# Zero rows by one write and two DMA copies, one weight piece ahead of the list reads, and one gather behind a weight piece

## The chip, the cores and the metric

The kernel runs on one core of one Trainium2 chip. The metric is the device time of one execution in microseconds (us), lower is better. Three executions of the kernel before took 493.13, 488.73 and 491.85 us; the median is 491.85 us.

## The reference

A gated linear attention (4 batches, 8 heads, 768 steps, head size 48) with a complex decay, and on its output, seen as 3072 tokens of 384 values, a mixture of 8 experts. Each token goes to one expert only:

```python
logits = x @ w_gate
e_idx = np.argmax(logits, axis=1)
...
for e in range(E):
    mask = e_idx == e
    h = np.maximum(x[mask] @ w1[e], 0.0)
    ye = h @ w2[e]
    out[mask] = gate_w[mask, None] * eom[mask, e, None] * ye
```

Here w1[e] is 384x1024 and w2[e] is 1024x384, both float32.

## The kernel before, in words

**Attention.** The 3072 tokens are 24 tiles of 128. A long text, `ORDER`, names every step of this part one by one (`sc.20.1`, `mk.20.1`, ...), and the instructions of all engines are recorded in that order; each engine then runs its own in that order and waits on semaphores. A tile's finished rows go to a table `xd` in DRAM (step `xs`, line 723, SP's queue).

**Routing.** In four batches the tokens get a place in their expert's list. `pl` computes addresses on POOL (GpSimd) with seven small operations (lines 1024 to 1031), `el` writes 20 of the 24 tiles' entries to a DRAM table by indirect DMA (line 1035). The last four tiles are placed in SBUF instead. The experts are taken in order of their size, so which expert comes first is known only at run time (`who`, a register on SP).

**Weights.** An expert's weights come in four pieces of 768 KB (`piece`, line 296: w1 first half, w2 first half, w1 second half, w2 second half) into three staging buffers `raw`. Each piece is split in three steps into a rounded high part (`w1h`, `w2h`, a cast on ACT) and the rest (`w1l`, `w2l`, a subtraction on DVE). A buffer is free for the next piece when DVE has done its third subtraction. All piece loads and all reads of the lists stand on SP's one queue, which waits at its head.

**Rows.** A gather (line 1089) is four indirect DMAs issued by POOL that bring an expert's token rows from `xd` into `rows[e % 2]`. Lists may be shorter than the room for them, so `open_` (line 783) first zeroes both `rows` tiles, four 128x384 memsets each on POOL (line 791). PE turns the rows (`transpose_x`), ACT and DVE split them into `xh` and `xl`.

**Experts.** For each expert `e` eight rounds `ft` follow. In a round PE makes 9 up products (line 1176, into bank `b` or `xo` by turns), ACT takes the relu `hh` (line 1272), DVE the rest `hl` (line 1273), and one round later PE makes 9 down products from them (line 1191). By hand-written numbers each round also takes some steps of a chain of work for the next expert (`steps`: six splits of the first expert's last two pieces, twelve splits of the second's, the issue of the third's pieces, three turned row tiles). In the first expert's rounds another chain (`last`, the function `lists`) enters the last four tiles into all experts' lists: compare rows `hot`, gates, a product (line 862) and its copy `by_slot`, then additions to `slots` and `whole`, the row numbers `sid`, and the second expert's gather. The lists of the experts 2 to 8 are read from DRAM by SP (`read_ranked`: six reads at line 1056, four at line 1062) just after the first expert's fourth piece is asked for. Line 1161 is the branch that picks a matmul width for an expert at run time; line 186 is the helper of all transposes.

Of the kernel before, what the change touches and what calls it, by code (L numbers as in the profile page):

```python
# [21 lines left out]
P = 128  # L22
# [85 lines left out]
va.19 xn.18v rnd.23a cq.20.0v xs.18 fr.23 dk.22 abs.23a st.19 qc.22 xt.19 sin.23 trk.20.0 sd.19 cos.23 trk.20.1  # L108
ck.20.0v cq.21.1 trq.22.0 cps.19v ck.20.1 ro.19 kc.21 cq.21.0 open set.16 sc.20.1 gt.19 qc.23 sc.20.0 mk.20.1
trk.21.0 R1.3 trk.21.1 ck.21.0 st.20 ck.21.1v rk.3 R3.3 sc.21.1 R2.3 Ae.3 sd.20 pl.3 sc.21.0 R4.3 cps.20 mk.21.1  # L110
st.21 el.3 mk.21.0 mk.20.0 trq.23.1 trq.23.0 kc.22 trq.22.1 kc.23 va.20 xn.19v K2 chk xs.19 trk.22.1 xt.20 sd.21
trk.23.1 cq.22.1 ck.22.1v va.21 cps.21 K3 ck.23.1 cq.22.0 K4 sc.22.1 xt.21 cq.23.1v KV trk.22.0 cq.23.0v
trk.23.0 mk.22.1 wd sc.23.1 ck.23.0 rr ck.22.0v lw.2 wr sc.23.0 mk.23.1 lw.0 sc.22.0 mk.23.0 ro.20 si mk.22.0 ga
ro.21 xh.20 gt.20 xn.20 xl.20 va.22 xh.21 xs.20 gt.21 P1.0 xn.21 xs.21 xl.21 st.22 xt.22v PK.0 sd.22 ro.22 P2.0
# [9 lines left out]
def tile_gated_attention_moe(  # L124
# [13 lines left out]
    nc = tc.nc  # L138
# [3 lines left out]
    HD = H * D  # L142
# [3 lines left out]
    N = B * S  # L146
# [140 lines left out]
    def one(w, e):  # L287
        return w[e] if isinstance(e, int) else w[bass.ds(e, 1)].rearrange("o a b -> (o a) b")

    def piece(stage, e, n, since=None):  # L290
        t = stage.tile([P, KT * FH], F32, name="raw")
        if n % 2 == 0:
            src = one(w1, e).rearrange("(k p) f -> p k f", p=P)[:, :, n // 2 * FH:(n // 2 + 1) * FH]
        else:
            src = one(w2, e).rearrange("(k p) f -> p k f", p=P)[:, n // 2 * TH:(n // 2 + 1) * TH, :]
        ins = nc.sync.dma_start(out=t.rearrange("p (k f) -> p k f", f=src.shape[2]), in_=src)
        if since is not None:
            behind(ins, since)
        return t
# [139 lines left out]
    def attention(wctx, pp):  # L439
        with ExitStack() as actx:  # L440
# [342 lines left out]
            def open_():  # L783
                ectx.close()
                ready["stage"] = wctx.enter_context(tc.tile_pool(name="stage", bufs=3, side="right", reuse_waits="tile"))
                pool = wctx.enter_context(tc.tile_pool(name="wset0", bufs=1, side="right", reuse_waits="tile"))
                ready["pool"], ready["set"] = pool, weight_set(pool)
                for n in range(2):
                    rows[n] = pool.tile([P, NS, HD], F32, name=f"rows{n}")
                    for i in range(NS):  # L790
                        nc.gpsimd.memset(rows[n][:, i, :], 0.0)
                for name, dt in (("dl", F32), ("oh", BF16), ("ohp", F32)):
                    tail[name] = pool.tile([P, NT - T0, E], dt, name=name + "s")
                ready["x"] = [pool.tile([P, KT, CAP], F32R, name=n) for n in ("xh0", "xl0")]

            def lw(n):
# [143 lines left out]
            def late():  # L940
# [11 lines left out]
                rk=rk, R2=R2, R3=R3, Ae=Ae, R4=R4, pl=pl, el=el, K1=K, K2=K, K3=K, K4=K, KV=K, chk=chk, wd=wd, wr=wr, open=open_,  # L952
                lw=lw, sa=sa, sb=sb, rr=rr, si=si, ga=ga, P1=PK, PK=PK, P2=PK, tl=tl, th=th, fl=fl, cn=cn, cv=cv)
            for name, f in (("y", y), ("z", z), ("u", u)):
# [25 lines left out]
            with tc.manual_schedule(engines={mybir.EngineType.SP, mybir.EngineType.Pool}):  # L980
                for name, a, moved in todo:
# [3 lines left out]
                    if whose:  # L985
                        left[whose] -= 1
                        if not left[whose]:
                            free.append(held[whose])
            for ins in read_ranked(1, E):
                behind(ins, tail["gathered"])  # L990
# [95 lines left out]

    def gather(e, cap, known=N, loaded=True):
        for i, (t, n) in enumerate(tiles_at(e, cap, loaded)):
            ins = nc.gpsimd.indirect_dma_start(  # L1089
                out=rows[e % 2][:n, i, :], out_offset=None, in_=xd[:known],  # L1090
                in_offset=bass.IndirectOffsetOnAxis(ap=id_of(e, i, n, loaded), axis=0),
                bounds_check=known - 1, oob_is_err=False)
        return ins


    def experts(ready, loaded=False):
# [4 lines left out]
        with ExitStack() as ectx:  # L1101
# [14 lines left out]
            turns_of = [*part, *hidden, sums, done_rows, *bank_of.values()]  # L1116
            X, W, L = {}, {}, {}

            def across(e, columns):
# [16 lines left out]
            def weights(e):  # L1136
                W[e] = wsets[e % 2]
                if e + 1 < E and e not in L:
                    L[e] = pieces_of(e)
# [109 lines left out]
            for e in range(E):  # L1249
                if e + 1 < E and not (loaded and e == 0):  # L1250
                    gather(e + 1, sizes[e + 1], loaded=loaded)
                steps = itertools.chain(ready["late"]() if loaded and e == 0 else (), ahead(e + 1))
                accs, cap = None, sizes[e]
                for ft in range(FT):
# [3 lines left out]
                    if loaded and e == 0 and ft < 2:  # L1258
                        if before is not None:
                            by_width(e, down_products(*before))  # L1260
                    elif loaded and e == 0 and ft == 3:
                        by_width(e, up_products(e, ft, up))
# [28 lines left out]
                    if loaded and e == 0:  # L1291
                        for _ in range((0, 2, 1, 0, 0, 0, 0, 0)[ft]):
                            next(last)
# [5 lines left out]
                        if ft >= 4:  # L1299
                            next(flags, None)  # L1300
                    for _ in range((0, 0, 4, 4, 4, 4, 3, 3)[ft] if loaded and e == 0 else 3):
                        next(steps, None)
# [221 lines left out]
```

## Time and profile before

| | |
|---|---|
| median of 3 runs | 491.85 us (488.73 to 493.13) |
| profiled execution, its own time | 492.66 us |
| its span, first to last instruction | 490.9 us |
| around the span | 1.76 us |
| mean granted TensorE clock | 0.990 |
| busy share PE, DVE, ACT, POOL | 95%, 70%, 62%, 27% |

The profile is one execution. Its views: a page with busy time by engine and by slice, the chain of waits that ended last, the timeline of each engine (start, duration, in brackets the idle time before and what ended it), and windows with each engine's busy time, the granted clock and the DMA engines' share. Attention ends near 250 us of the span, the first expert's rounds run from there to about 282 us, the other seven experts to 482 us.

### The profile page before, as it was taken

To read this page: it belongs to the slowest core of one execution; us is meant where nothing else is said; L and a number is where in the kernel's file an instruction comes from. 1 tells how busy PE (TensorE), PEld (TensorE's weight loads), DVE (VectorE), ACT (ScalarE), POOL (GpSimd) and SP (SyncE) were. 2 spreads that over 40 slices of the span, in tenths; PEclk is the share of its full clock that TensorE was granted. 3 is DMA by queue.
4 is the path that set the end of the run, shared out by engine and by line. 5 is a ranking of instruction groups with operands and counts; after the bars stand their busy time and mean duration, and the time that the engine had idled before them with its cause. 6 is when DMAs were issued, how large, how long until landed. Compare 5 with 4: busy or idle time off the path is not lost.

```text
span 490.9 us, 11411 instructions
## 1 busy us (share of the span) xinstructions
PE 465.4 (95%) x4350; PEld 419.6 (85%) x4350; DVE 342.7 (70%) x694; ACT 303.5 (62%) x569; POOL 132.4 (27%) x168
## 2 busy tenths in 40 slices
PE   8998999899999999989899789999999999999991
PEld 4786777788988789879799689999999999999991
DVE  4599999999999999998798564272644527283210
ACT  7759889989997987542536464372744636283330
POOL 5100000013700640582404543324241322011112
PEclk9999999999999999998999999999999999999997
DMA  8974354534633331002636996274452827220001
GB/s 278 316 232 132 99 159 126 168 91 102 122 129 99 78 72 50 18 4 76 229 86 221 241 246 200 63 229 131 138 180 51 284 61 232 80 91 26 22 27 49
DMA packets 46829, 64.28 MB, mean 131 GB/s; under 512 B 11679, under 2 KB 38570, under 8 KB 46740
## 3 DMA queue, kind: packets, MB, share of 16 engines
q1 hardware_dynamic: 38612, 53.63, 36.6%
q0 software_dynamic: 8128, 9.42, 6.9%
q8 instruction: 62, 1.02, 0.8%
q14 instruction: 27, 0.22, 0.2%
HBM read 53.92 MB, written 9.88 MB: 130 GB/s over the span
## 4 chain that ended last, share of the span: by engine, by line
PE 64%; DVE 23%; ACT 5%; DMA 3%; issue 3%; SPq 0%; POOL 0%; POOLq 0%; DVEq 0%; ACTq 0%
PE b L1191 11%; PE b L1176 10%; PE xo L1176 9%; PE b L186 7%; PE st L1191 6%; PE b L665 4%; DVE scores L670 3%; PE xo L697 2%; PE b L335 2%; DVE qc L642 2%; DVE kc L642 2%; PE xo L703 2%; PE b L610 2%; PE st L854 2%; PE b L1223 2%
## 5 line engine op out<-in xcount | busy, mean ns | idle before, releaser
L1210 POOL DMA_INDIRECT out_dram<-y,sid x28 | 33.3, 1190 | 126.7 <-ACT y L1232 123.8
L665 PE MATMUL b<-qt,kt 96*128 96x128 f32 x384 | 48.3, 279 | 1.5 <-ACT qt L654 1.1
L665 PEld LDWEIGHTS b<-qt,kt 96*128 96x128 f32 x384 | 44.9, 192 | 5.3 <-ACT qt L654 1.8
L1089 POOL DMA_INDIRECT rows<-xd,sid x28 | 34.4, 1228 | 48.5 <-DVE gate L1072 24.4
L1273 DVE SCALAR_TENSOR_TENSOR hl<-b,hh 128x464 fp32r<-128x464 f32 (+7 forms) x32 | 18.9, 590 | 40.7 <-ACT hh L1272 40.7
L1273 DVE SCALAR_TENSOR_TENSOR hl<-xo,hh 128x464 fp32r<-128x464 f32 (+7 forms) x32 | 18.8, 588 | 39.6 <-ACT hh L1272 39.6
L1272 ACT ACTIVATE hh<-b 128x464 fp32r<-128x464 f32 (+7 forms) x32 | 16.6, 518 | 40.3 <-PE b L1176 39.0
L1191 PE MATMUL b<-hh,w2l 128*128 128x392 f32 (+6 forms) x112 | 38.5, 343 | 1.1 <-issue 1.1
L582 POOL COPY rcs<-rcs 24x48 f32<-24x48 f32 (+2 forms) x10 | 7.7, 775 | 114.4 <-DMA rcs<-re 72.7
L1191 PE MATMUL b<-hh,w2h 128*128 128x392 f32 (+6 forms) x112 | 38.5, 344 | 0.0
L1272 ACT ACTIVATE hh<-xo 128x464 fp32r<-128x464 f32 (+7 forms) x32 | 16.6, 520 | 34.1 <-PE xo L1176 33.2
L697 PE MATMUL xo<-scores,v 128*48 128x128 f32 x384 | 37.2, 283 | 0.4 <-DVE scores L670 0.4
L1176 PE MATMUL xo<-xh,w1h 128*128 128x392 f32 (+6 forms) x93 | 32.8, 353 | 1.6 <-issue 1.6
L1176 PE MATMUL b<-xh,w1h 128*128 128x392 f32 (+6 forms) x93 | 33.6, 361 | 0.2 <-issue 0.2
L1035 POOL DMA_INDIRECT table<-entry,addr x20 | 28.2, 1409 | 18.1 <-DVE scores L670 11.6
L670 DVE TENSOR_TENSOR scores<-b,mask 128x512 f32<-128x512 f32 x48 | 31.6, 678 | 1.0 <-PE b L665 0.9
L703 PE MATMUL xo<-qt,state 96*48 96x128 f32 x320 | 32.0, 278 | 0.0
L1176 PE MATMUL b<-xl,w1h 128*128 128x392 f32 (+6 forms) x93 | 31.6, 340 | 0.0
L1176 PE MATMUL xo<-xl,w1h 128*128 128x392 f32 (+6 forms) x93 | 31.6, 340 | 0.0
L1176 PE MATMUL xo<-xh,w1l 128*128 128x392 f32 (+6 forms) x93 | 31.6, 340 | 0.0
L1176 PE MATMUL b<-xh,w1l 128*128 128x392 f32 (+6 forms) x93 | 31.6, 339 | 0.0
L315 DVE TENSOR_TENSOR w1l<-raw,w1h 128x512 fp32r<-128x512 f32 x42 | 26.6, 686 | 5.9 <-ACT w1h L314 5.9
(282 smaller groups left out, 1325.8 us busy)
## 6 DMA issues: line engine op xcount, KB each, us to landing
raw<-in_moe_w_dram SPq DMA_DIRECT2D x32, 768.0 KB
ar<-in_a_re_dram SPq DMA_DIRECT2D x24, 192.0 KB
ai<-in_a_im_dram SPq DMA_DIRECT2D x24, 192.0 KB
q<-in_q_dram SPq DMA_DIRECT2D x24, 192.0 KB
k<-in_k_dram SPq DMA_DIRECT2D x24, 192.0 KB
v<-in_v_dram SPq DMA_DIRECT2D x24, 192.0 KB
xd<-xn SPq DMA_DIRECT2D x24, 192.0 KB
rows<-xd,sid POOLq DMA_INDIRECT x28, 7.0
```

The source lines that it names most:

```text
L186: return nc.tensor.transpose(out=out, in_=in_, identity=ident[p0:p0 + n, p0:p0 + n])
L665: nc.tensor.matmul(sp[:, j * P:(j + 1) * P], cats_t["k"][i % 2][:D2, h, :], cats_t["q"][i % 2][:D2, h, :], start=True, stop=True)
L670: nc.vector.tensor_tensor(out=scores[i % 2][:, 4 * hh:4 * hh + 4, :], in0=of(("sc", i, hh)).rearrange("p (h t) -> p h t", t=P), in1=mask.u ...
L697: nc.tensor.matmul(op[u * DP:u * DP + D, j * P:(j + 1) * P], vt[:, h * D:(h + 1) * D], scores[i % 2][:, h, :], start=True, stop=(cc == 0))
L703: nc.tensor.matmul(op[u * DP:u * DP + D, j * P:(j + 1) * P], xs[:D2, h * D:(h + 1) * D], cats_t["q"][i % 2][:D2, h, :], start=False, stop= ...
L1035: ins = nc.gpsimd.indirect_dma_start(out=table, out_offset=bass.IndirectOffsetOnAxis(ap=addr[:, c:c + 1], axis=0), in_=entry[:, c, :], in_ ...
L1089: ins = nc.gpsimd.indirect_dma_start(out=rows[e % 2][:n, i, :], out_offset=None, in_=xd[:known], in_offset=bass.IndirectOffsetOnAxis(ap=id ...
L1176: nc.tensor.matmul(used(up[:, :sizes[e]], n), w[:, kt, :], used(x[:, kt, :], n), start=(m == 0), stop=(m == 3 * KT - 1))
L1191: nc.tensor.matmul(used(accs[kt][:, :sizes[e]], n), w[:, cs], used(a, n), start=(ft == 0 and s == 0), stop=(ft == FT - 1 and s == 2))
L1210: ins = nc.gpsimd.indirect_dma_start(out=out, out_offset=bass.IndirectOffsetOnAxis(ap=id_of(e, i, n, loaded), axis=0), in_=y[:n, :], in_of ...
L1272: nc.scalar.activation(out=hh, in_=up[:, :cap], func=AF.Relu)
L1273: nc.vector.scalar_tensor_tensor(out=hl, in0=up[:, :cap], scalar=0.0, in1=hh.bitcast(F32), op0=ALU.max, op1=ALU.subtract)
```

## The change

What it does: (1) POOL zeroes one 128x384 block of `rows[0]`; two DMAs on SP's queue copy it into the other three blocks of `rows[0]` and the four of `rows[1]` (new step `zr`, right behind `open`). (2) The first expert's third piece (`lw.2`) is asked for behind its first and second, not ahead of them. (3) The second expert's first piece is asked for ahead of the list reads; its other three stay behind them. (4) The third expert's gather waits until the second expert's fourth piece has landed. (5) In the first expert's rounds the splits begin one round earlier, and three of the four steps of `last` come one round later (the product of line 862 in round 3, the additions and the second expert's gather in round 4).

```diff
@@ -106,11 +106,11 @@
-ck.20.0v cq.21.1 trq.22.0 cps.19v ck.20.1 ro.19 kc.21 cq.21.0 open set.16 sc.20.1 gt.19 qc.23 sc.20.0 mk.20.1
+ck.20.0v cq.21.1 trq.22.0 cps.19v ck.20.1 ro.19 kc.21 cq.21.0 open zr set.16 sc.20.1 gt.19 qc.23 sc.20.0 mk.20.1
-trk.23.0 mk.22.1 wd sc.23.1 ck.23.0 rr ck.22.0v lw.2 wr sc.23.0 mk.23.1 lw.0 sc.22.0 mk.23.0 ro.20 si mk.22.0 ga
+trk.23.0 mk.22.1 wd sc.23.1 ck.23.0 rr ck.22.0v wr sc.23.0 mk.23.1 lw.0 sc.22.0 mk.23.0 ro.20 si mk.22.0 ga lw.2
@@ -287,6 +287,8 @@
     def one(w, e):
         return w[e] if isinstance(e, int) else w[bass.ds(e, 1)].rearrange("o a b -> (o a) b")
+    issued = []
+
     def piece(stage, e, n, since=None):
         t = stage.tile([P, KT * FH], F32, name="raw")
         if n % 2 == 0:
@@ -294,6 +296,7 @@
         else:
             src = one(w2, e).rearrange("(k p) f -> p k f", p=P)[:, n // 2 * TH:(n // 2 + 1) * TH, :]
         ins = nc.sync.dma_start(out=t.rearrange("p (k f) -> p k f", f=src.shape[2]), in_=src)
+        issued.append(ins)
         if since is not None:
             behind(ins, since)
         return t
@@ -787,11 +790,15 @@
                 ready["pool"], ready["set"] = pool, weight_set(pool)
                 for n in range(2):
                     rows[n] = pool.tile([P, NS, HD], F32, name=f"rows{n}")
-                    for i in range(NS):
-                        nc.gpsimd.memset(rows[n][:, i, :], 0.0)
+                nc.gpsimd.memset(rows[0][:, 0, :], 0.0)
                 for name, dt in (("dl", F32), ("oh", BF16), ("ohp", F32)):
                     tail[name] = pool.tile([P, NT - T0, E], dt, name=name + "s")
                 ready["x"] = [pool.tile([P, KT, CAP], F32R, name=n) for n in ("xh0", "xl0")]
+
+            def zr():
+                nought = lambda n: rows[0][:, 0:1, :].broadcast_to([P, n, HD])
+                nc.sync.dma_start(out=rows[0][:, 1:, :], in_=nought(NS - 1))
+                nc.sync.dma_start(out=rows[1], in_=nought(NS))
             def lw(n):
                 for x in (0, 1) if n == 0 else (n,):
@@ -950,7 +957,7 @@
                 dk=dk, dq=dq, rcs=rcs, rcp=rcp, rt=rt, rcc=rcc, cdma=cdma, car=car, cp=cp, rnd=rnd, fr=fr, abs=abs_, sin=sin,
                 cos=cos, sc=sc, mk=mk, st=st, sd=sd, cps=cps, va=va, xt=xt, ro=ro, xn=xn, gt=gt, xs=xs, xh=xh, xl=xl, R1=R1,
                 rk=rk, R2=R2, R3=R3, Ae=Ae, R4=R4, pl=pl, el=el, K1=K, K2=K, K3=K, K4=K, KV=K, chk=chk, wd=wd, wr=wr, open=open_,
-                lw=lw, sa=sa, sb=sb, rr=rr, si=si, ga=ga, P1=PK, PK=PK, P2=PK, tl=tl, th=th, fl=fl, cn=cn, cv=cv)
+                lw=lw, sa=sa, sb=sb, rr=rr, si=si, ga=ga, P1=PK, PK=PK, P2=PK, tl=tl, th=th, fl=fl, zr=zr, cn=cn, cv=cv)
             for name, f in (("y", y), ("z", z), ("u", u)):
                 steps[name + "a"] = lambda *a, f=f: f(*a, below)
                 steps[name + "b"] = lambda *a, f=f: f(*a, above)
@@ -986,6 +993,7 @@
                         left[whose] -= 1
                         if not left[whose]:
                             free.append(held[whose])
+            ready["second"] = [piece(ready["stage"], who[1], 0)]
             for ins in read_ranked(1, E):
                 behind(ins, tail["gathered"])
             ups, accs = [of(("ua", 0, 0)), op], [state_sum] + [of(("th", kt)) for kt in range(1, KT)]
@@ -1084,12 +1092,14 @@
     def gate_of(e, i, n, loaded=True):
         return whole[:n, i, 1:2] if loaded and e == E - 1 else gate[:n, e, i:i + 1]
-    def gather(e, cap, known=N, loaded=True):
+    def gather(e, cap, known=N, loaded=True, since=()):
         for i, (t, n) in enumerate(tiles_at(e, cap, loaded)):
             ins = nc.gpsimd.indirect_dma_start(
                 out=rows[e % 2][:n, i, :], out_offset=None, in_=xd[:known],
                 in_offset=bass.IndirectOffsetOnAxis(ap=id_of(e, i, n, loaded), axis=0),
                 bounds_check=known - 1, oob_is_err=False)
+            for x in since if i == 0 else ():
+                behind(ins, x)
         return ins
@@ -1115,6 +1125,7 @@
             bank_of = {n: Turns(ps, n, [P, 512], b, tiles=kept.get(n)) for n, b in (("up", 2), ("xt", 2), ("yp", 1), ("acc", KT))}
             turns_of = [*part, *hidden, sums, done_rows, *bank_of.values()]
             X, W, L = {}, {}, {}
+            last_piece = []
             def across(e, columns):
                 if e < E - 1:
@@ -1135,7 +1146,10 @@
             def weights(e):
                 W[e] = wsets[e % 2]
-                if e + 1 < E and e not in L:
+                if loaded and e == 1:
+                    L[e] = ready["second"] + [piece(stage, who[e], n) for n in range(1, 4)]
+                    last_piece.append(issued[-1])
+                elif e + 1 < E and e not in L:
                     L[e] = pieces_of(e)
                 yield from split_pieces(L.pop(e), W[e])
                 if e + 1 < E:
@@ -1248,7 +1262,7 @@
             flags = over(lpool, bank_of["yp"].next, more_than) if loaded else None
             for e in range(E):
                 if e + 1 < E and not (loaded and e == 0):
-                    gather(e + 1, sizes[e + 1], loaded=loaded)
+                    gather(e + 1, sizes[e + 1], loaded=loaded, since=last_piece if e == 1 else ())
                 steps = itertools.chain(ready["late"]() if loaded and e == 0 else (), ahead(e + 1))
                 accs, cap = None, sizes[e]
                 for ft in range(FT):
@@ -1258,7 +1272,7 @@
                     if loaded and e == 0 and ft < 2:
                         if before is not None:
                             by_width(e, down_products(*before))
-                    elif loaded and e == 0 and ft == 3:
+                    elif loaded and e == 0 and ft in (3, 4):
                         by_width(e, up_products(e, ft, up))
                         next(last)
                         by_width(e, down_products(*before))
@@ -1289,7 +1303,7 @@
                             for i in range(len(last_tiles)):
                                 down_rows(e, accs, i, *h)
                     if loaded and e == 0:
-                        for _ in range((0, 2, 1, 0, 0, 0, 0, 0)[ft]):
+                        for _ in range((0, 1, 1, 0, 0, 0, 0, 0)[ft]):
                             next(last)
                         if ft == 1:
                             _, values = nc.values_load_multi_w_load_instructions(
@@ -1298,7 +1312,7 @@
                             now["spare"].update(enumerate(values))
                         if ft >= 4:
                             next(flags, None)
-                    for _ in range((0, 0, 4, 4, 4, 4, 3, 3)[ft] if loaded and e == 0 else 3):
+                    for _ in range((0, 3, 3, 4, 3, 3, 3, 3)[ft] if loaded and e == 0 else 3):
                         next(steps, None)
                     next(put_next, None)
                 for _ in steps:
```

POOL at the end of the third batch's entries, before and now (`rows` are the two zeroed tiles, the `row` operation after them begins the addresses of the last DRAM batch):

```order
L1031 TENSOR_SCALAR addr_127<-row_2695 128x6
L1035 DMA table_64<-entry_128,addr_127 3712x2 x6
L791 MEMSET rows0_2847 128x384 x4
L791 MEMSET rows1_2852 128x384 x4
L1024 TENSOR_SCALAR row_2939<-rank_125 128x2
```

```order
L1039 TENSOR_SCALAR addr_127<-row_2695 128x6
L1043 DMA table_64<-entry_128,addr_127 3712x2 x6
L793 MEMSET rows0_2847 128x384
L1032 TENSOR_SCALAR row_2934<-rank_125 128x2
L1033 TENSOR_SCALAR row_2934<-row_2934 128x2
```

Seven of eight memsets left POOL. On SP the two copies stand between two of the `xd` writes (tiles 18 and 19), ahead of the register load of the experts' order and of the first list read:

```order
L726 DMA xd_63<-xn0_208 128x384
L800 DMA rows0_2847<-rows0_2847 128x3x384
L801 DMA rows1_2848<-rows0_2847 128x4x384
L726 DMA xd_63<-xn1_209 128x384
L433 TENSOR_LOAD order_148
L1064 ISA
L1064 DMA slots_134<-table_64 116x8
```

SP from the first expert's fourth piece on, before and now (`slots` and `whole` are the list reads; before, raw_3372 is that fourth piece and raw_3729 the second expert's first; now they are raw_3367 and raw_3414):

```order
L296 DMA raw_3372<-in_moe_w2_dram 128x4x384
L1056 ISA
L1056 DMA slots_134<-table_64 110x8
...
L1062 DMA whole_136<-table_64 32x3x2
L296 ISA
L296 DMA raw_3729<-in_moe_w1_dram 128x3x512
L1161 UNCONDITIONAL_BRANCH x3
L296 ISA
L296 DMA raw_3731<-in_moe_w2_dram 128x4x384
```

```order
L298 DMA raw_3367<-in_moe_w2_dram 128x4x384
L298 ISA
L298 DMA raw_3414<-in_moe_w1_dram 128x3x512
L1064 ISA
L1064 DMA slots_134<-table_64 110x8
...
L1070 DMA whole_136<-table_64 32x3x2
L1175 UNCONDITIONAL_BRANCH x2
L298 ISA
L298 DMA raw_3698<-in_moe_w2_dram 128x4x384
```

One piece moved past ten list reads. ACT in the first expert's rounds, before and now (raw_3111 and raw_3139 are the first expert's third piece, `exs` and `ens` belong to the gates):

```order
L1272 ACTIVATE hh1_3458<-xo_216 128x464
L328 ACTIVATE exs_3496<-dls_2857 128x32
L1161 UNCONDITIONAL_BRANCH
L328 ACTIVATE ens_3498<-loss_3494 128x4
L1161 UNCONDITIONAL_BRANCH
L1272 ACTIVATE hh2_3459<-b1_211 128x464
L865 COPY by_slot_3607<-b0_210 24x464
L806 CAST w1h1_2841<-raw_3111 128x512
L1161 UNCONDITIONAL_BRANCH
L806 CAST w1h1_2841<-raw_3111 128x512 x2
L806 CAST w2h1_2845<-raw_3372 128x512
L1272 ACTIVATE hh3_3460<-xo_216 128x464
```

```order
L1286 ACTIVATE hh1_3455<-xo_216 128x464
L813 CAST w1h1_2841<-raw_3139 128x512 x3
L1175 UNCONDITIONAL_BRANCH x2
L1286 ACTIVATE hh2_3456<-b1_211 128x464
L331 ACTIVATE exs_3593<-dls_2850 128x32
L331 ACTIVATE ens_3595<-loss_3591 128x4
L813 CAST w2h1_2845<-raw_3367 128x512 x3
L1175 UNCONDITIONAL_BRANCH x2
L872 COPY by_slot_3655<-b0_210 24x464
L1286 ACTIVATE hh3_3457<-xo_216 128x464
L317 CAST w1h0_3444<-raw_3414 128x512 x3
L317 CAST w2h0_3448<-raw_3698 128x512
```

The splits of the third and fourth piece stand ahead of `by_slot` now, and the second expert's first piece is split in the round of `hh3`.

## Rows read from the trace of the kernel before

**Rows 1.** Page: the span, then busy us, share and count by engine.

```profile
span 490.9 us, 11411 instructions
PE 465.4 (95%) x4350; PEld 419.6 (85%) x4350; DVE 342.7 (70%) x694; ACT 303.5 (62%) x569; POOL 132.4 (27%) x168
```

**Rows 2.** Windows, 220 to 278: length, busy (count) by engine, PE clock, DMA share, GB/s.

```profile
220.00:222.00 2.00, 2.00 (x16) 1.27 (x16) 2.00 (x4) 0.00 (x0) 1.24 (x4) 0.84 0.00 0
222.00:224.00 2.00, 2.00 (x22) 1.98 (x20) 1.85 (x6) 0.00 (x0) 1.66 (x2) 0.50 0.03 6
224.00:226.00 2.00, 2.00 (x22) 1.67 (x18) 0.77 (x2) 0.84 (x2) 0.00 (x0) 0.81 0.26 94
...
276.00:278.00 2.00, 0.70 (x4) 0.69 (x5) 1.18 (x3) 1.83 (x4) 1.37 (x1) 1.00 1.15 180
```

**Rows 3.** Timeline, 215 to 220: start, us, engine, line, operation, count, [idle before, releaser].

```profile
215.75 2.96 POOL L791 MEMSET rows<- 128x384 f32 x8
215.93 2.79 DVE L403 TENSOR_SCALAR en<-en 128x2 f32<-128x2 f32 x1
219.77 1.97 PE L186 MATMUL b<-ident,qc 128*96 128x128 f32 x12 [1.98 <-DVE scores L670]
```

**Rows 4.** Chain of waits, 216 to 227: start, us, what.

```profile
216.01 2.73 DVE en L403
...
221.73 0.60 PE xo L697 x4
...
225.10 1.01 PE b L186 x8
...
226.47 0.22 PE xo L703 x4
```

**Rows 5.** Timeline of DVE, its first wait behind the stall.

```profile
225.23 0.55 DVE L685 TENSOR_TENSOR state<-st,rc 96x384 f32<-96x384 f32 x1 [1.24 <-PE xo L703]
```

**Rows 6.** Timeline of SP and DVE, 248 to 262: the list reads and pieces.

```profile
248.73 0.41 SPq L296 DMA_DIRECT2D raw<-in_moe_w_dram  x1
249.38 2.85 SPq L1056 DMA_DIRECT2D slots<-table  x6
252.41 3.24 SPq L1062 DMA_DIRECT2D whole<-table  x4
255.90 0.41 SPq L296 DMA_DIRECT2D raw<-in_moe_w_dram  x1
261.97 0.39 SPq L296 DMA_DIRECT2D raw<-in_moe_w_dram  x1
250.07 1.28 DVE L810 TENSOR_TENSOR w2l<-raw,w2h 128x512 fp32r<-128x512 f32 x2
```

**Rows 7.** Chain of waits, then timelines of ACT and PE, 267 to 280.

```profile
267.88 8.27 DMA raw<-in_moe_w_dram
...
279.31 0.39 PE b L186 x4
...
276.17 0.62 ACT L314 CAST w2h<-raw 128x512 fp32r<-128x512 f32 x1 [2.47 <-DMA raw<-in_moe_w_dram]
...
277.30 0.46 PE L1191 MATMUL st<-hh,w2h 128*128 128x432 f32 x1 [1.38 <-ACT hh L1272]
```

**Rows 8.** Gathers of the second and the third expert: last issue, times to landing.

```profile
267.80 1.59 POOL L1089 DMA_INDIRECT rows<-xd,sid  x1 [0.31 <-issue]
...
DMA to landing us min/median/max: 5.9/5.9/5.9
...
DMA to landing us min/median/max: 12.9/14.4/16.0
```

**Rows 9.** Chain, nine up products; timeline of PE, two waits for nothing the profile shows.

```profile
254.28 2.03 PE b L1176 x9
...
289.14 0.35 PE L1191 MATMUL b<-hh,w2l 128*128 128x408 f32 x1 [1.07 <-issue]
295.59 0.45 PE L1176 MATMUL xo<-xh,w1h 128*128 128x408 f32 x1 [1.56 <-issue]
```

## The prediction, on record before the changed kernel was run

> **What bounds the kernel now.** The page says first who is full: TensorE (PE) is busy for 465.4 of 490.9 us [rows 1], so 25.5 us are idle and the rest can only shrink where PE runs slowly. A change like this one, which leaves every matmul in place, can win nothing but idle time and lost clock. The windows and the timeline of PE say where these lie in the stretch that the change touches, from the zeroing of the rows to the second expert's rounds; the chain of waits says which of them set the end.
>
> Three places count. **First, the zeroing.** The eight memsets on POOL run from 215.75 to 218.71. A DVE operation on 128x2 numbers that starts at 215.93 takes 2.79 us and ends at 218.72, together with the last memset [rows 3]. It stands in the chain with 2.73 us [rows 4], so PE is waiting for it: PE's next transposes come after 1.98 us of idleness that ended with a DVE operation [rows 3]. Then PE's clock falls: 0.84, 0.50, 0.81 in the windows from 220 to 226 [rows 2], between its two levels of 2.4 and 1.2 GHz. **Second, the second expert's fourth piece.** Asked for at 267.88, it lands 8.27 us later; ACT, which has waited 2.47 us for it, makes the relu only behind that cast, and PE stands still for 1.38 us [rows 7]. **Third,** PE waits 1.07 and 1.56 us for nothing that the profile shows [rows 9].
>
> **The change part by part.**
>
> Zeroing. One memset takes 2.96/8 = 0.37 us [rows 3]; it ends near 216.2, so the DVE operation does too, 2.5 us earlier than 218.72. PE's gap of 1.98 us is smaller than these 2.5 and goes whole: **1.98 us**. If the gap goes, I expect the full clock. The eight groups of four products from 221.73 to 225.10 took 3.37 us; at full clock such a group takes 0.22 us [rows 4], eight of them 1.76, which is 1.61 less. The windows say about the same: 0.16 + 0.50 + 0.19 of two us each are 1.7 us of lost clock [rows 2]. Since a first group also pays for its start, I take **1.5 us**. DVE does not cap the sum: at 225.23 it had waited 1.24 us for PE [rows 5], so with its own 2.5 us it can be 3.7 earlier. Part one is 1.98 + 1.5, or 3.5 us. Its ends are 2.0 (the clock falls all the same) and 3.7.
>
> The two copies. They move seven blocks of 192 KB. No row shows a copy from SBUF to SBUF. The nearest is the window 224 to 226, in which one 192 KB store was moved: 0.26 of 2 us, 0.52 us of all DMA engines [rows 2], so 3.6 us for seven; from the slowest window, 180 GB/s [rows 2], 1.38 MB take 7.6 us. I take 3.6, the row that ran without company. From 216.2 that ends between 220 and 224, while the DMA engines stand at 0.00 and 0.03 [rows 2]. Behind the copies SP's queue holds the store of tile 19, the register load and the list read; the first gather needs all of these anyway. Cost 0; without that cover, with 7.6 us for the copies, they would end at 223.8 and hold up the store of the window 224 to 226, then due 3.5 us earlier, by up to 3.3 us. POOL loses 2.6 us of work that nothing waits for.
>
> The first expert's third piece behind its first two: three loads asked for in a row, in another order; the two that are split first land first. 0 us.
>
> The second expert's first piece, now ahead of the list reads. Its buffer is free when DVE ends its subtraction at 251.35; it was asked for only at 255.90, behind ten list reads that take from 249.38 to 255.65 [rows 6]. It moves up 4.5 us. The reads move back by the 2.4 us from 249.4 to about 251.8 and end near 258.1; one of the last four shares a semaphore with the new load and waits until it has landed, which I estimate at a few tenths. The second piece, at 261.97 held back by its buffer, can go at about 258.4 now that the splits begin a round earlier: 3.5 us earlier. The third and the fourth follow by the same 3.5, so the fourth lands near 276.15 - 3.5 = 272.6. ACT's wait of 2.47 us is shorter than that, and PE's **1.38 us** go.
>
> What is late next: the second expert's rows. Their gather comes one round later. Nine products take 2.03 us [rows 9], so a round is at most 4 us; DVE is less crowded at the new place, and I count 2.6 to 3.6 us. Its last DMA, issued at 267.80 with a landing time of 5.9 us [rows 8], then lands between 276.3 and 277.3 (in the old clock). PE turns these rows from about 279.3 [rows 7], and 1.38 earlier without its gap: 277.9. That is a margin of 0.6 to 1.6 us, less than a slow landing would take. Part two is between 0 and 1.4; I take 1.0.
>
> The product on the lists waits for the gates, and three more subtractions of 0.64 us [rows 6] stand ahead of these on DVE, 1.9 us; but PE has nine more products, 2.03 us [rows 9], ahead of it as well. 0 us, at worst some tenths.
>
> The third expert's gather waits for that fourth piece on POOL; behind it stand the fourth expert's gather and the first expert's stores. The second's gather issues until about 272, the piece lands at 272.6: no wait to speak of, at most 3.5 us if the piece lands as late as before. Its rows are turned five rounds into the second expert, some 20 us on, more than the 16.0 us of its slowest landing [rows 8]. 0 us.
>
> PE's two unexplained waits, 2.63 us together [rows 9], lie behind the stretch in which the DMA engines are full: 1.15 in the window 276 to 278 [rows 2]. About a piece less is then outstanding. They can go, stay, or grow by as much; I take 0.5 us of gain.
>
> **Sum:** 3.5 + 1.0 + 0.5 = 5.0 us. Against the profiled execution's own 492.66 (span 490.9 and 1.76 around it) that is 487.7; it ran 0.8 above the median of the three runs, well inside their spread. Against that median of 491.85 it is **486.9 us**. A measurement of this kernel can tell about 1%, 4.9 us, from no change, so the forecast lies on that edge.
>
> **The rivals.**
>
> *The clock falls anyway.* For it: the work ahead of the gap is made of small matmuls. Against it: the gap of 1.98 us is the longest here, and after 1.38 us at 277 the windows still show 1.00 [rows 2, 7]. It costs the 1.5: 488.4 us. Chance 0.18.
>
> *The stall is not the memsets'.* That one DVE operation is held through eight memsets is odd [rows 3]: with its turn after the first it would have lost 0.4 us, and the other 2.3 would have another cause and remain. Then part one is gone and 1.0 + 0.5 are left: 490.4 us. Against it: start and end fit the whole train to 0.2 us [rows 3]. Chance 0.05. The Trainium skill (SBUF — State Buffer, section Who interferes with whom) says that whichever of DVE and GpSimd issues first gets the shared port pair for the whole instruction, and the other blocks fully. By that rule, read to the letter, DVE comes in after one memset, and the time is this rival's; the trace, with its 2.79 us, does not agree.
>
> *The DMA engines are relieved more than I think.* The gaps of 2.63 go whole, 2.1 more than I took: 484.8 us. For it: the loads start earlier, in a stretch where the engines had room. Against it: the second expert's rounds load as much as before. Chance 0.16.
>
> *Slower: the second expert's rows come too late.* Its gather now falls among three pieces. If it lands as slowly as the third expert's did, 16.0 us [rows 8], the last of it lands at 271.4 + 16.0 = 287.4 against a need at 277.9: PE waits 9.5 us. With 3.5 + 1.4 won that is 491.85 + 4.6 = 496.5 us. It decides from a landing time of about 11 us on; up to there the kernel is no slower than before. Against it: the load that met the third's gather is spread out by the change. Chance 0.04.
>
> **How the numbers follow.** My own case has 0.55, with 485.4 to 488.4 from the ends of its terms; 0.02 is left for what I don't see. The range from 484.3 to 490.5 takes in the first three rivals and leaves out the slow one and the far ends. Faster by over 1% (below 486.9): half of my case and the relieved engines, with a little taken off, 0.43. Slower by over 1%: 0.04. Within 1%: 0.53.
>
> **What would show it.** A DVE operation of some 0.3 us at 216 and no PE gap behind it; the granted clock at 1.00 from 218 to 228; the zero copies ended before the list read; the second expert's four pieces landed some 3.5 us earlier in relation to PE's rounds, and no PE wait in the first expert's last rounds; the second expert's transposes with no wait for rows. I would be wrong if the clock fell all the same, if the transposes waited for rows, or if PE's unexplained waits grew.

## The result, and the profile after

The changed kernel took 486.55 us (median of 18 runs, 483.94 to 488.99), the kernel before beside it 491.89 us (18 runs). The ratio is 0.9896, 95% interval 0.9873 to 0.9919. The forecast was 486.9. A second measurement (c_after, chip 10) gave 0.9931 (0.9894 to 0.9967), but a third (c_after_2, chip 6) 0.9996 (0.9967 to 1.0026). So the gain was there twice and missing once, and the last section says how far that could be followed. The rows here come from the first measurement, where the profiled execution took 486.38 us.

The page, first part (the span, then busy us, share and count by engine), answers to [rows 1]: 6.3 us less span, 1.8 of them off PE's own busy time.

```profile
span 484.6 us, 11407 instructions
PE 463.6 (96%) x4350; PEld 419.4 (87%) x4350; DVE 340.8 (70%) x694; ACT 303.5 (63%) x569; POOL 132.4 (27%) x161
```

The zeroing, timeline of all engines from 215 to 219 us (start, us, engine, line, operation), answers to [rows 3, 5]:

```profile
215.91 0.46 POOL L793 MEMSET rows<- 128x384 f32 x1
216.11 0.28 DVE L406 TENSOR_SCALAR en<-en 128x2 f32<-128x2 f32 x1
216.40 0.73 SPq L800 DMA_DIRECT2D rows<-rows  x1
217.18 1.82 SPq L801 DMA_DIRECT2D rows<-rows  x1
217.90 1.30 PE L186 MATMUL b<-ident,qc 128*96 128x128 f32 x10
```

DVE's operation takes 0.28 us in place of 2.79, and PE's next transposes carry no bracket: the 1.98 us are gone. The windows (length, busy time and count of PE, PEld, DVE, ACT, POOL, then PE's clock, DMA share, GB/s) answer to [rows 2]:

```profile
218.00:220.00 2.00, 2.00 (x24) 1.82 (x26) 2.00 (x3) 0.00 (x0) 1.32 (x3) 1.00 0.89 313
220.00:222.00 2.00, 2.00 (x31) 1.81 (x28) 1.86 (x7) 0.65 (x2) 1.33 (x2) 1.00 0.96 339
222.00:224.00 2.00, 2.00 (x35) 1.77 (x33) 1.83 (x8) 1.79 (x4) 0.00 (x0) 1.00 0.36 107
224.00:226.00 2.00, 2.00 (x20) 1.85 (x17) 1.97 (x6) 0.59 (x1) 0.00 (x0) 1.00 0.00 0
...
274.00:276.00 2.00, 0.95 (x8) 0.54 (x6) 0.62 (x2) 0.95 (x2) 1.61 (x1) 1.00 0.91 276
276.00:278.00 2.00, 1.71 (x9) 1.52 (x10) 1.13 (x2) 0.53 (x1) 1.61 (x1) 0.83 0.45 96
278.00:280.00 2.00, 2.00 (x7) 1.96 (x6) 0.00 (x0) 0.01 (x1) 1.61 (x2) 0.50 0.51 95
```

From 218 to 224 the clock is full and the copies run: (0.89 + 0.96 + 0.36) x 2 = 4.4 us of all DMA engines, the store of tile 19 (asked for at 220.80) among it. From 224 to 226 their share is 0.00, and SP asks for the first list read at 225.13. But from 276 to 280 the clock now is 0.83 and 0.50, where before it was full. PE had just turned the second expert's rows. Its timeline there (in brackets the idle time before, and what ended it), and from the chain the last row DMA and the first groups of nine products, answer to [rows 7 to 9]:

```profile
273.81 0.45 PE L186 MATMUL b<-ident,rows 110*128 110x110 f32 x3
274.47 0.69 PE L186 MATMUL b<-ident,rows 110*128 110x110 f32 x5 [0.21 <-DMA rows<-xd,sid]
276.05 0.60 PE L186 MATMUL b<-ident,rows 110*128 110x110 f32 x4 [0.89 <-DVE xl L1144]
```

```profile
267.06 7.37 DMA rows<-xd,sid
...
276.88 3.01 PE b L1190 x9
...
282.11 1.66 PE xo L1190 x9
```

The last row DMA lands 7.37 us after its issue and PE waits 0.21 us for it; nine up products then take 3.01 us, 1.35 more than the next nine. The gap of 1.38 us ahead of these transposes is gone, and so are the waits of 1.07 and 1.56 us. SP asks for the second expert's pieces at

```profile
247.69 0.40 SPq L298 DMA_DIRECT2D raw<-in_moe_w_dram  x1
255.06 0.40 SPq L298 DMA_DIRECT2D raw<-in_moe_w_dram  x1
257.90 0.39 SPq L298 DMA_DIRECT2D raw<-in_moe_w_dram  x1
260.55 0.37 SPq L298 DMA_DIRECT2D raw<-in_moe_w_dram  x1
```

against 255.90 for the first before [rows 6] and 267.88 for the fourth [rows 7]; ACT casts the fourth without a wait:

```profile
266.55 0.62 ACT L317 CAST w2h<-raw 128x512 fp32r<-128x512 f32 x1
```

**Stages.** The table cuts each trace at five PE rows: the transposes after a wait of some 0.37 us near 167 us, the first expert's first up product (S1 ends), the second expert's first row transposes (S2), its first up product (S3), its sixth group of up products (S4); the rest is 187.0 to 187.7 us in every trace. "Full" is the DMA share of the 7.5 us after the second expert's first product, "waits" PE's idle time in S4 that nothing in the profile explains. c_before, c_after and c_after_2 are the two kernels unedited, measured again; the other labels are explained with the experiments. Stages are compared within the first four rows or within the other ten: these ten were taken on three chips on which every trace has a late start near 170 us, in S1 (last section).

| kernel, label | ratio to before (95%) | S1 | S2 | S3 | S4 | full | waits |
|---|---|---|---|---|---|---|---|
| before | | 80.04 | 31.91 | 2.65 | 21.88 | 0.99 | 2.63 |
| after | 0.990 (0.987, 0.992) | 76.10 | 30.35 | 3.07 | 20.36 | 0.55 | 0 |
| before, c_before | | 78.75 | 32.04 | 2.65 | 21.62 | 0.94 | 2.36 |
| after, c_after | 0.993 (0.989, 0.997) | 75.99 | 30.30 | 3.93 | 18.82 | 0.58 | 0 |
| after, c_after_2 | 1.000 (0.997, 1.003) | 81.13 | 30.29 | 3.54 | 20.36 | 0.59 | 0 |
| e1_zero_alone | 1.003 (1.000, 1.006) | 83.87 | 31.41 | 2.75 | 19.66 | 0.97 | 0.59 |
| e6_zero_again | 1.003 (1.000, 1.007) | 82.99 | 31.80 | 2.76 | 21.54 | 0.90 | 2.16 |
| e8_zero_third | 1.003 (1.000, 1.007) | 81.16 | 31.82 | 2.76 | 21.43 | 0.91 | 2.07 |
| e5_other_kind | 1.003 (0.999, 1.006) | 83.81 | 31.92 | 2.66 | 19.96 | 0.89 | 0.80 |
| e2_rest_alone | 0.999 (0.996, 1.003) | 81.55 | 30.29 | 2.95 | 18.85 | 0.56 | 0 |
| e7_rest_again | 0.996 (0.994, 0.999) | 83.83 | 30.27 | 3.74 | 20.08 | 0.54 | 0 |
| e3_no_hold | 1.001 (0.998, 1.004) | 82.89 | 30.29 | 3.43 | 18.85 | 0.51 | 0 |
| e4_piece_behind_reads | 1.001 (0.997, 1.005) | 82.93 | 30.30 | 3.74 | 18.82 | 0.52 | 0 |
| v1_rows_earlier | 0.999 (0.996, 1.002) | 81.19 | 30.26 | 2.77 | 21.61 | 0.95 | 2.26 |

The profiled pair differs by 3.94 + 1.56 - 0.42 + 1.52 us in the four stages, less 0.17 ahead and 0.16 behind them: 6.27 us, the difference of the spans. The second pair's stages differ by 2.76 + 1.74 - 1.28 + 2.80 = 6.02 us. There the changed kernel was 2.70 us behind at 167 us already, which no instruction of the change can make (a wait of 0.67 us for POOL at 79 and a low clock at 94).

### The profile page after: what moved, and what is told of

The parts are those of the page before. It is cut to its first block, busy times and chain, and to the rows that moved or that the text cites. A ratio compares the mean times of both kernels' runs of the same rounds, so it can differ in the third digit from the quotient of the medians.

```text
span 484.6 us, 11407 instructions
## 1 busy us (share of the span) xinstructions
PE 463.6 (96%) x4350; PEld 419.4 (87%) x4350; DVE 340.8 (70%) x694; ACT 303.5 (63%) x569; POOL 132.4 (27%) x161
## 4 chain that ended last, share of the span: by engine, by line
PE 63%; DVE 21%; DMA 5%; ACT 4%; issue 4%; POOL 0%; SPq 0%; POOLq 0%; DVEq 0%; ACTq 0%
PE b L1205 12%; PE b L1190 10%; PE xo L1190 10%; PE b L186 6%; PE st L1205 6%; DVE scores L673 3%; PE b L668 3%; DMA rows<-xd,sid 3%; DVE kc L645 2%; DVE qc L645 2%; PE b L338 2%; PE b L613 2%; PE st L861 2%; PE b L1237 2%; PE b L562 2%
## 5 line engine op out<-in xcount | busy, mean ns | idle before, releaser
L1097 POOL DMA_INDIRECT rows<-xd,sid x28 | 35.8, 1279 | 45.9 <-DVE gate L1080 27.1
L585 POOL COPY rcs<-rcs 24x48 f32<-24x48 f32 (+2 forms) x10 | 8.7, 875 | 113.7 <-DMA rcs<-re 76.9
L700 PE MATMUL xo<-scores,v 128*48 128x128 f32 x384 | 36.2, 277 | 0.4 <-DVE scores L673 0.4
```

The source lines that it names most:

```text
L700: nc.tensor.matmul(op[u * DP:u * DP + D, j * P:(j + 1) * P], vt[:, h * D:(h + 1) * D], scores[i % 2][:, h, :], start=True, stop=(cc == 0))
L1097: ins = nc.gpsimd.indirect_dma_start(out=rows[e % 2][:n, i, :], out_offset=None, in_=xd[:known], in_offset=bass.IndirectOffsetOnAxis(ap=id ...
```

## Experiments

**The four parts.** First, the zeroing by itself (e1), all the rest by itself (e2), and the change without one of its parts (e3, e4). No run separates the place of `lw.2`, the earlier splits and the later steps of `last`.

```diff
e1, e6, e8: before, zeroing alone
-                    for i in range(NS):
-                        nc.gpsimd.memset(rows[n][:, i, :], 0.0)
+                nc.gpsimd.memset(rows[0][:, 0, :], 0.0)
+            def zr():
...
e2, e7: the change, with before's memsets (no zr)
e3: the change without the hold of the third expert's gather
-gather(e + 1, sizes[e + 1], loaded=loaded, since=last_piece if e == 1 else ())
+gather(e + 1, sizes[e + 1], loaded=loaded, since=())
e4: the change, first piece behind the list reads
-            ready["second"] = [piece(ready["stage"], who[1], 0)]
             for ins in read_ranked(1, E):
                 behind(ins, tail["gathered"])
+            ready["second"] = [piece(ready["stage"], who[1], 0)]
```

> The kernel before, with the change of the zeroing alone: one memset and two copies by DMA; pieces, rounds and gathers as before. Theory: up to the first up products of the first expert the two traces stand 3.63 us apart (247.23 against 243.60), and the zeroing made all of it; the gap of 1.38 us before the second expert and the two waits for nothing the profile shows (2.63 us) belong to the other parts of the change and stay. That gives 491.9 - 3.6 = 488.3 us, with no low clock near 221. Rival one: the two waits come of how PE's rounds fall against the transfers, so that any shift removes them: 485.7 us. Rival two: a low clock of 3.41 us, which costs 1.7, turns up elsewhere: 490.0 us.

> The changed kernel with the eight memsets of before on POOL and no copies: pieces, rounds and gathers of the change alone. Theory: DVE's operation of 2.79 us and the low clock near 221 are back (3.6 us); the gap of 1.38 us is gone, the second expert's transposes wait some tenths for rows, and the two waits of 2.63 us are gone, since they belong to this part: 486.55 + 3.6 = 490.2 us, and 488.6 if the low clock near 277 comes only in company with part one. Rival: the two waits go with part one and stay here: 492.8 us.

> The changed kernel without the order that holds the third expert's gather behind the second expert's last piece. Theory: that piece has landed by 266.1, before POOL is through with the second expert's gather at 270, so the hold holds nothing: 486.5 us, within 0.3. Rival: the hold is what spreads the transfers and so removed the two waits of 2.63 us; they come back: 489.2 us.

> The changed kernel with the second expert's first piece asked for behind the ten list reads again. Theory: the reads end about 1 us earlier, which nothing waits for (the product on the lists is bound by PE's rounds); the first piece is asked for some 6 us later and lands about 1.5 us after ACT could cast it; the following pieces move by about as much, which ACT's idle 1.5 and 2.0 us before the last two relus take up: 486.5 to 487.2 us. Rival one: the early piece is what removed the gap of 1.38 us and relieved the DMA engines: 488 to 489 us. Rival two: the piece ahead of the reads makes the second expert's gather late and so the clock fall; without it 485.0 us.

All four times missed the expectations (495.48, 493.64, 493.93 and 494.08 us against 492.92 for before), because each trace is 5 to 8 us longer in S1 than after's, and 3.3 to 5.8 of that is lost by 185 us, ahead of everything the change touches. The later stages answer all the same. **Hold:** S2 to S4 of e3 are those of the change: it holds nothing. **First piece:** e4's S2 and S4 are too: asking for the first piece ahead of the list reads is worth nothing that these stages show. **Pieces and rounds:** with this part S2 is 30.3 us, without it 31.4 to 32.0; the waits stand only without it. So what gains 1.6 us in S2 and up to 2.7 in S4 (21.54 in e6 against 18.85 in e2 and e3) is what e2, e3 and e4 have in common: `lw.2` behind the first two pieces, the splits a round earlier, three steps of `last` a round later, and the moved loads and gathers that follow from them.

e2 also shows what the memsets hold and what not, in one stretch of the timeline:

```profile
220.30 2.97 POOL L794 MEMSET rows<- 128x384 f32 x8
220.41 0.17 DVE L397 TENSOR_REDUCE los<-lo 128x2 f32<-128x16 f32 x1
221.70 0.17 DVE L377 TENSOR_TENSOR rk<-oh,b 128x16 f32<-128x16 bf16 x1 [1.13 <-PE b L374]
221.99 0.54 DVE L688 TENSOR_TENSOR state<-st,rc 96x384 f32<-96x384 f32 x1
222.46 0.15 DVE L405 TENSOR_REDUCE sm<-ex 128x2 f32<-128x16 f32 x1
222.53 0.77 DVE L406 TENSOR_SCALAR en<-en 128x2 f32<-128x2 f32 x1
```

Reduces and TENSOR_TENSOR run beside the memsets at their usual length; TENSOR_SCALAR waits for the last one's end (223.27). It came 2.2 us into the train, lost 0.6 us, and PE shows no wait there. So the stall of before is a meeting: 2.79 us if the operation comes as the train begins, little if it comes late.

**The same programs unedited.**

> The changed kernel once more, nothing edited, in another session. The four experiments before all show a stretch near 170 us, ahead of anything that the change touches, in which DVE and SP receive TensorE's signal 4 us late, and a low clock some 12 us behind it; the two traces of before and after do not have it. Theory one: it belongs to the session or the chip and hits every kernel; then this one has it as well, takes about 493 us, and its ratio to before tells what the change is worth where both have it. Theory two: it belongs to the four edited programs; then this one takes 486.5 us, and the ratio to before is 0.99 again.

> The kernel before once more, nothing edited, in the same session as the changed one. Theory one (the late signal near 170 us belongs to the session or the chip): it stands in this trace as well, and the time is about 493 us or, if before has been free of it so far at 491.9 us, 497. Theory two (it belongs to the edited programs): 491.9 us and a trace as before.

Neither trace had the late signal: 487.6 and 492.03 us, beside 490.32 for before (so before measured against itself reads 1.002). Theory two looked right; the pair below shows that the late signal needs no edit. c_before adds one thing. It has the same gap of 1.98 us, and the clock behind it stays full:

```profile
219.73 1.51 PE L186 MATMUL b<-ident,qc 128*96 128x128 f32 x9 [1.98 <-DVE scores L670]
```

```profile
220.00:222.00 2.00, 2.00 (x22) 1.40 (x22) 2.00 (x4) 0.00 (x0) 1.24 (x4) 1.00 0.00 0
222.00:224.00 2.00, 2.00 (x34) 1.81 (x29) 1.86 (x7) 0.50 (x2) 1.62 (x2) 1.00 0.04 11
```

And c_after waits longer for the rows, 1.06 us, with no low clock behind it:

```profile
277.72 0.50 PE L186 MATMUL b<-ident,rows 110*128 110x110 f32 x3 [1.06 <-DMA rows<-xd,sid]
```

**Held by kind, and the rows earlier.**

```diff
e5: before, for the group of two tiles alone
-        nc.vector.tensor_scalar(out=en, in0=en, scalar1=1.0, scalar2=None, op0=ALU.add)
-        nc.vector.scalar_tensor_tensor(out=en, in0=sm, scalar=1e-9, in1=en, op0=ALU.add, op1=ALU.mult)
+        if n == 2:
+            nc.vector.scalar_tensor_tensor(out=en, in0=en, scalar=1.0, in1=sm, op0=ALU.add, op1=ALU.mult)
+        else:
...
v1: the change, in the first expert's rounds
                     elif loaded and e == 0 and ft in (3, 4):
+                        if ft == 4:
+                            next(last)
                         by_width(e, up_products(e, ft, up))
-                        next(last)
+                        if ft == 3:
+                            next(last)
...
-                    for _ in range((0, 3, 3, 4, 3, 3, 3, 3)[ft] if loaded and e == 0 else 3):
+                    for _ in range((0, 3, 3, 1, 6, 3, 3, 3)[ft] if loaded and e == 0 else 3):
```

> The kernel before with its eight memsets on POOL; DVE's held operation (the sum of a scalar, TENSOR_SCALAR on 128x2) is folded into the one behind it (SCALAR_TENSOR_TENSOR on two inputs), for this one group alone. Theory: in the run of the pieces and rounds alone, reduces, TENSOR_TENSOR and one operation of this kind ran in their usual 0.15 to 0.55 us while the memsets ran, and only the TENSOR_SCALAR was held to their end; so with the kind changed nothing is held, the gap of 1.98 us goes though POOL does what it did, and the time is that of the zeroing alone, some 3 us under before (ratio 0.993). Rival: whatever DVE issues there is held, or the next TENSOR_SCALAR is: a stall of 2.8 us stays and the ratio is 1.00.

> The kernel before with the change of the zeroing alone, as once before, in another session, since the first run had the late signal near 170 us ahead of the place. Theory: without that signal the gap of 1.98 us goes; 1.38 and the two waits at 289 and 295 stay or nearly so; ratio 0.993 (3.6 us under before), 0.996 if the low clock only moves to another place. Rival: the zeroing alone is worth nothing, as the first run's 1.003 says.

> The changed kernel with the eight memsets, pieces, rounds and gathers of the change alone, as once before, in another session. Theory: without the late signal DVE's operation falls into the memsets again and is held some 2.8 us; the gap of 1.38 us and the two waits are gone, some tenths to one us of waiting for rows are new: 2 to 4 us under before, ratio 0.993 to 0.996. Rival: the two waits go with any shift and are not this part's: ratio 0.998 or over.

> The changed kernel with the transposes of the lists ahead of the fifth round's up products and three of the fourth round's steps a round later, so that the second expert's gather is asked for some 1.7 us earlier. Theory: TensorE's wait for those rows, 0.21 to 1.06 us in four runs with this order, goes, and with it a cause of the low clock behind it: 0.2 to 1.1 us under the changed kernel, up to 2.7 where that one's clock fell there; ratio to before 0.986 to 0.990. Rival: the wait only turns into one for the splits, which come a round later: the same time as the changed kernel.

The late signal was there again (495.72, 495.65, 492.77 and 493.80 us, before 493.36), so the times of e5 and e6 say nothing on what a full stall would cost. e5's rows do answer the question of the kind: the eight memsets run, and the folded operation (which leaves out the 1e-9 added to `sm`) runs among them in 0.16 us.

```profile
222.67 2.96 POOL L794 MEMSET rows<- 128x384 f32 x8
225.10 0.16 DVE L404 SCALAR_TENSOR_TENSOR en<-en,sm 128x2 f32<-128x2 f32 x1
```

The Trainium skill (SBUF — State Buffer, section Who interferes with whom) says that tensor_scalar can contend with GpSimd for the shared ports, that reduces never do, and that two-input operations do so only with a GpSimd instruction that reads SBUF. These rows agree for every operation seen; of the two-input ones only e5's has both inputs in SBUF, those of e2 read one (`b`, `st`) from PSUM. They do not agree that the lock lasts for one instruction: 2.79 us of holding is eight memsets of 0.37 us, not one.

v1 was meant to beat the change and did not. PE no longer waits for rows (S3 is 2.77), but the two unexplained waits are back:

```profile
280.55 0.92 PE L186 MATMUL b<-ident,rows 110*128 110x110 f32 x8
...
283.32 0.42 PE L1190 MATMUL b<-xh,w1h 128*128 128x408 f32 x1 [0.36 <-issue]
290.84 0.45 PE L1205 MATMUL b<-hh,w2l 128*128 128x408 f32 x1 [1.62 <-issue]
296.85 0.45 PE L1190 MATMUL xo<-xh,w1h 128*128 128x408 f32 x1 [0.64 <-issue]
```

Three splits went a round later to make room, so pieces behind them went later too: counted back from the second expert's first product, its fourth piece is asked for at 12.3 us (16.3 in after, 13.9 in before). But the third expert's gather moved as well, and the other way: it begins 9.8 us ahead of that product (6.6 in after, 12.1 in before). The DMA engines are full again when the second expert starts, as they are in before and as they are not in the change; which of the two moves fills them is not shown. Windows over the first 7.5 us of its products, v1, before and after:

```profile
283.32:290.82 7.50, 5.90 (x30) 5.48 (x30) 4.50 (x8) 4.91 (x11) 3.98 (x4) 1.00 0.95 210
```

```profile
281.79:289.29 7.50, 6.43 (x33) 6.10 (x34) 4.48 (x8) 5.01 (x11) 4.09 (x4) 1.00 0.99 214
```

```profile
276.88:284.38 7.50, 7.50 (x32) 7.30 (x33) 2.96 (x5) 3.50 (x8) 5.20 (x5) 0.77 0.55 139
```

The table has this for 14 traces: all seven with a share of 0.89 or more have the waits, all seven with 0.59 or less have none. How full engines make PE wait is not shown.

**The changed kernel and the zeroing alone, on one chip.**

> The changed kernel once more, nothing edited, beside an edited one on the same chip. Eight edited programs on two chips have TensorE's late signal near 170 us, and four runs of before and of the change have not, which were on other chips. Theory one (it belongs to the chip): both kernels of this pair have it or both have not; where both have it, this one takes about 494 us and its ratio to before is near 1.00. Theory two (it belongs to the edited programs): this one takes 486 to 488 us without it, ratio 0.990 to 0.993, and the edited one has it.

> The kernel before with the change of the zeroing alone, a third time, beside the unedited changed kernel. Where the late signal near 170 us is missing: the gap of 1.98 us goes, 488 to 489 us, ratio 0.993 to 0.996, and the gap of 1.38 us and some of the two later waits stay. Where it stands: 495.5 us as twice before, ratio 1.003.

Both traces have the late signal: 493.43 and 495.39 us beside 492.99 for before. Theory two fails: the same unedited program had the late signal here and had not twice before. That it belongs to the chip alone, whatever the program, is not shown. Before took 492.92, 493.36 and 492.99 us on the three chips, only 1.0 to 1.5 above its 491.89 in the first measurement, while the changed kernel rose by 6.9; so before may well have lost less there. Between the two programs of this pair the pieces and rounds are still worth something: 2.0 us of the time, and 1.5 in S2 and 1.1 in S4, less 0.8 in S3.

## Why the prediction was right, and where its working was not

The number was right, 486.9 against 486.55, in part by luck: two of its terms were not right, and their errors cancel. Two of the three signs that the prediction itself named for being wrong came true, a low clock and transposes that wait for rows.

**Zeroing, 1.98 us: right.** Operation and gap are as forecast in both pairs that have a trace of before. S1 fell by 2.76 us in the pair without a low clock there; that also holds 0.43 us for which c_before waited for the first expert's rows. No run has the zeroing alone where the stall stands, so its worth rests on S1 of these pairs.

**The clock, 1.5 us: the step that failed.** "If the gap goes, I expect the full clock" held where the gap had been, but the term was booked as a gain of the whole run. In the profiled pair it was taken at 221 and lost again at 277, and the mean granted clock of the two traces is the same, 0.990; S4 is 20.36 us in that trace and 18.82 in c_after at full clock, 1.5 less. The gap is no sure cause either: c_before had it without a low clock, and after had a low clock with shorter idle times. "The clock falls anyway" (0.18) came true for the profiled execution, at a place that it did not name, and not for that of c_after.

**The copies, 0 us: right.** At most 4.4 us of DMA time in place of 3.6, below the bound of 7.6, and done before the first list read.

**Pieces, 1.38 us: right.** The fourth is asked for 7.3 us earlier, 3.6 of it beyond the 3.77 by which PE reaches the first up product earlier (247.23 and 243.46; the expectation of e1 has 3.63 from 243.60, the chain's figure), where 3.5 were forecast. It also landed faster, within 6.0 us against 8.27. The gain came with the rounds; the place ahead of the reads, on which the step spent most of its words, moved nothing that could be measured (e4).

**Rows: forecast a margin of 0.6 to 1.6 us, measured a wait of 0.21 (after), 1.06 (c_after) and 0.59 us (c_after_2).** The landing was sized at 5.9 us [rows 8] and took 7.37. Part two with it came to 1.56 - 0.42 = 1.1 us in S2 and S3, 1.0 forecast.

**The unexplained waits, 0.5 us: mis-sized.** They went whole, 2.63 us [rows 9] and 2.36 in the second pair. "The DMA engines are relieved more than I think" (0.16) is what happened. The reason named for it, loads that start earlier, fits the traces, but it is not shown: e4 rules out the first piece, and v1 moved the last pieces and a gather at once.

**The hold, 0 us: right** (e3).

The range allowed for nothing like the late signal: the 493.43 us of c_after_2 lie outside it.

## What to carry to other kernels

An operation that is odd for its length beside a train of short ones on POOL can be freed from either side: take the train away, or give the operation a kind that does not wait. A low clock behind a gap is not a term to add to the gap; of two traces of one kernel one may have it and the other not. And where DMA engines are full as a stage begins, look at what was asked for before it: by moving three splits later and a gather earlier v1 gained 0.2 to 1.2 us in S3 and lost 2.8 in S4, against the traces of the change that have no low clock there. Last, measure a change on more than one chip: here its ratio was 0.990, 0.993 and 1.000.

## What the hardware showed that was not expected

On three chips (5, 6 and 8) operations that wait for a group of 48 small products start late, as if TensorE's signal came late. In one of these traces DVE starts the operation that reads the products of 169.54 at 173.73, after 3.23 us of waiting, though PE had ended them at 170.42 by its own rows (c_after_2, timelines of PE and DVE; the bracket names a later product, which by its row ended at 173.05):

```profile
169.54 0.88 PE L683 MATMUL st<-v,kc 128*32 128x48 f32 x48
173.73 0.56 DVE L688 TENSOR_TENSOR state<-st,rc 96x384 f32<-96x384 f32 x1 [3.23 <-PE b L613]
175.27 0.64 PE L186 MATMUL b<-ident,qc 128*96 128x128 f32 x4 [1.35 <-ACT ri L331]
```

In the first trace of after the same operation starts as those products end:

```profile
168.87 0.55 DVE L688 TENSOR_TENSOR state<-st,rc 96x384 f32<-96x384 f32 x1
```

All ten traces from these chips have it, with waits of 2.5 to 4.0 us, six of them with a low clock between 176 and 184 us; the four others (before, after, c_before, c_after) have not. Why it comes late is not shown. With S1 shifted so, DVE's operation comes 2.2 us into the memsets (0.77 and 0.78 us in e2 and e7), so the zeroing has little left to win there. Why the zeroing alone, and the change of the kind alone, are 0.3% slower than before on these chips (for the latter the interval includes no change) stays open: no trace of before was taken on one of them.
